# A decay attention with a gated feed-forward behind it: softmax bias taken straight from a masked minimum, remainders moved to VectorE, first half tile spread, last tile in one chain

## The chip, the core and the metric

The kernel runs on one core of a Trainium2 chip. The core has five engines with queues of their own: TensorE (PE in the profile, its weight loads PEld), VectorE (DVE), ScalarE (ACT), GpSimd (POOL) and SyncE (SP), which here only issues DMAs. The metric is the time on the device of one execution, in microseconds (us).

## What is computed

Eight batches with eight heads each, 576 positions, 64 values per head. Attention has a decay (a running sum of log f) added to the scaled scores, a causal mask, a softmax and a product with v. The result, laid out as 4608 rows of 512 values, goes through a two-layer network with hidden width 2048.

```python
scores = scale * np.matmul(q, k.transpose(0, 1, 3, 2))
decay = cum[:, :, :, None] - cum[:, :, None, :]
scores = np.where(causal, -1000000000.0, scores + decay)
scores = scores - np.max(scores, axis=-1, keepdims=True)
attn = np.exp(scores)
attn = attn / (np.sum(attn, axis=-1, keepdims=True) + 1e-09)
x = matmul(attn, v)            # then as rows of 512
h = x @ w_in
g = h * np.clip(h + 3.0, 0.0, 6.0) / 6.0
out = g @ w_out
```

Matrix products of 16-bit operands are made to hold more digits by splitting an operand into a high and a low half (`hi` is the value rounded to 16 bits, `lo` the remainder), so that each product is three matmuls.

## The kernel before

**Work items.** Attention goes through a list `VH`: four items of kind A (batch 0, two heads each, the first 256 positions), eight of kind B (batch 0, the other positions of one head), and 56 of kind F (one head each of batches 1 to 7). Kind F is the function `rows`. For one head it works in two halves (chunks 1, 4 and 0 of the rows, then chunks 2 and 3). A half goes like this: TensorE writes scores to `pn` (L611, L614); VectorE adds the mask, writes `pp` and takes each row's maximum into `mc`, a tile `MF` (L622, a multiply-reduce followed by a read of the accumulator); VectorE makes the exponent's bias `nb` = -max/8 + log(16) in a pass of its own (L628); ScalarE takes exp with that bias (L634) and rounds the result to 16 bits into a buffer `ring` (L651); the remainders are subtractions into the same buffer (L654 for the columns left of the last two blocks, L660 and L665 for what is in front of them, called "the pair" and "the corner" below); SyncE issues a transposing DMA to `pT` (L672). For batch 1 the remainder of chunk 3 stands on GpSimd (`PL_POOL`), for batches 2 to 7 the pairs and the corner do (`B0_POOL`). A head later `av` multiplies `pT` with v into `pav` (L697 to L702; L708 for kinds A and B), divides by the row sums (L726, L729, L732, for batch 0 also L731), splits into halves `xhl` (L737, L738), and `x_move` issues transposing DMAs to `xT` and `xS`.

**Network.** A tile `t` of 512 rows (one batch less 64 rows, which are put together in `xS`) is sixteen units `h_unit` and four units `out_unit`. An `h_unit` is 12 matmuls to `ph` (L786 to L788), then ScalarE `r` (L794), VectorE `r` (L797, the last to read `ph`), ScalarE `gT` high (L798) and VectorE `gT` low (L799). An `out_unit` is 48 matmuls to `po` (L839 to L841), a scaled copy to `o` on ScalarE (L845) and DMAs to the result (L848). Tile 0 is done in two halves of 256 rows: the first after kind A, the second after kind B. `h_short` and a last `out_unit` do the rows in `xS`; for the last batch these are two units of 256 columns with their operand in `vst`.

**Order.** The network's units are generators in a queue; `fill` gives them credit, eight times in each work item, at a rate that is `F_RATE[0]` in kind B, `F_RATE[1]` in batch 1 and follows from what is left after that. Credit sets the place in the written program. A scheduler that goes by its own estimates then orders each engine's instructions, with the place in the written program as the priority; engines run their queues in that order. `behind` tells it to put a matmul after one named before it (used for the last tile's `h_unit`s). In PSUM two buffers hold `pn` and `ps` (tag S), two hold `ph` and `po` (tag mm) and a third is lent to them.

Of the kernel before, what the change touches and what calls it, by code (L numbers as in the profile page):

```python
# [11 lines left out]
F32 = mybir.dt.float32  # L12
# [3 lines left out]
ALU = mybir.AluOpType  # L16
# [4 lines left out]
def kernel(  # L21
# [60 lines left out]
    NQK, NL, NST = 3, 2, 3  # L82
    W_RATE = (8, 2, 4)
    H_COST = 1.05
    F_RATE = (0.6, 0.45)
    PIN = 0
    PIN0 = 1
    LOW_W = 0
# [9 lines left out]
    VH += [("F", n) for n in range(H, NHEAD)]  # L98
    NV = len(VH)
    NRING = 3  # L100
    PL_POOL = ((3, ), ())
    NAT = ((1, 4, 0), (2, 3))
    B0_POOL = ((0, 0), (1, 1))
    W_AHEAD = (4, 5)
    W_ORDER = 0
    POOL_REST = ((0, 0, 0, 0), (0, 0, 0, 0))
# [484 lines left out]
    ringh = [t.bitcast(F16) for t in ring]  # L591
    clean = set()

    def rows(v):
        i, j = v % NQK, v % NL
        n = VH[v][1]
        late = min(n // H, 2) - 1
        pT = p2.tile([P, 3200], F16, tag="PHL", name=f"pT_{v}")
        mc = MF[v % 2]
        nb = p2.tile([P, NCH], F32, tag="nb", name=f"nb_{v}")  # L600
        e0 = 0
        for half in range(2):
            pn = ps_s.tile([P, 1024], F32, tag="S", name=f"pn_{v}_{half}")
# [15 lines left out]
            for x, c in enumerate(NAT[half]):  # L619
                o, r, kw = PLACE[c], RR[c], RB[c] + RR[c]  # L620
                at[c] = w
                nc.vector.tensor_tensor_reduce(  # L622
                    pp[:r, w:w + kw], pn[:r, o:o + kw], W[:r, 4 * P + r - kw:4 * P + r],
                    1.0, -3.0e38, ALU.add, ALU.max, accum_out=mc[:r, e0 + x:e0 + x + 1],
                )
                w += kw
            e1 = e0 + len(NAT[half])
            nc.vector.tensor_scalar(  # L628
                nb[:, e0:e1], mc[:, e0:e1], -0.125, math.log(PSC), op0=ALU.mult, op1=ALU.add
            )  # L630
            for x, c in enumerate(NAT[half]):
                r, kw = RR[c], RB[c] + RR[c]
                x_ = pp[:r, at[c]:at[c] + kw]
                nc.scalar.activation(  # L634
                    x_, x_, AF.Exp, bias=nb[:r, e0 + x:e0 + x + 1], scale=0.125
                )
            e0 = e1
            yield
# [1 line left out]
            def pair(t, a, b):  # L640
                return t[:, a:a + 2 * (b - a)].rearrange("p (n w) -> p n w", n=2)[:, :, 0:64]
# [6 lines left out]
                    clean.add(slot)  # L648
            for c in NAT[half]:
                r, kw, a = RR[c], RB[c] + RR[c], GH[half][c]  # L650
                nc.scalar.copy(hl[:r, h0[c]:h0[c] + kw], pp[:r, at[c]:at[c] + kw])  # L651
                if c:
                    eng = nc.gpsimd if c in PL_POOL[late] else nc.vector
                    eng.tensor_tensor(  # L654
                        hl[:r, a:a + c * P], pp[:r, at[c] + 64:at[c] + kw],
                        hl[:r, h0[c] + 64:h0[c] + kw], op=ALU.subtract,
                    )
            eng = nc.gpsimd if B0_POOL[late][half] else nc.vector
            a, b = NAT[half][:2]
            eng.tensor_tensor(  # L660
                pair(hl, h0[a] - 64, h0[b] - 64), pair(pp, at[a], at[b]), pair(hl, h0[a], h0[b]),
                op=ALU.subtract,
            )
            if 0 in NAT[half]:
                eng.tensor_tensor(  # L665
                    hl[:64, h0[0] - 64:h0[0]], pp[:64, at[0]:at[0] + 64], hl[:64, h0[0]:h0[0] + 64],
                    op=ALU.subtract,
                )

            w = sum((2 * c + 1) * P for c in NAT[half])  # L670
# [14 lines left out]
    def av(v, ph):  # L685
# [146 lines left out]

    def out_unit(s, three, col, rows_, gs=None, cols=(0, DM)):
        g = gT if gs is None else gs
        c = slice(*cols)
        po = mm_tile(f"po_{rows_[0]}_{cols[0]}", three)[:, c]
        ts_ = slice(s * P, (s + 1) * P)
        for fc in range(NFC):
            nc.tensor.matmul(po, g[:, 0, fc, ts_], w2[:, fc, 0, c], start=(fc == 0), stop=False)  # L839
            nc.tensor.matmul(po, g[:, 0, fc, ts_], w2[:, fc, 1, c], start=False, stop=False)  # L840
            nc.tensor.matmul(po, g[:, 1, fc, ts_], w2[:, fc, 0, c], start=False, stop=(fc == NFC - 1))  # L841
# [3 lines left out]
        nc.scalar.activation(o[:, c], po, AF.Copy, scale=scol(col))  # L845
        w = P // len(rows_)
# [248 lines left out]
```

## Time and profile before

| | us |
|---|---|
| median of 3 runs | 1079.81 (1077.97 to 1083.37) |
| the profiled execution, its own time | 1077.53 |
| its span, first to last instruction | 1075.5 |
| PE, DVE, ACT, POOL busy | 1011.0, 746.1, 588.6, 498.6 |

A row of the profile names line, engine, operation, tiles and shape, then count, busy time and mean duration of one in nanoseconds (ns), then the idle time of the engine just before, with what ended it. In the view of stages a row has the stretch in us from the span's start, each engine's busy time in it with its count, the granted TensorE clock as a share (PEclk), the DMA engines' share and GB/s. In the list of waits a row gives who waited for whom: us in total, times, longest. A matmul counts as busy from issue to its modelled end, so that back-to-back matmuls overlap.

### The profile page before, as it was taken

How to read it: one execution, taken by the hardware profiler on the slowest of the kernel's cores; microseconds unless marked ns; L12 is line 12 of the kernel's file. 1: busy time of each engine (PE TensorE's matmuls, PEld its weight loads, DVE VectorE, ACT ScalarE, POOL GpSimd, SP SyncE). 2: the span in 40 equal slices, each digit the busy share in tenths (PEclk: the TensorE clock that was granted, in tenths of full speed). 3: DMA queues.
4: the chain of work that ended last, by engine and by line, in shares of the span. 5: the costliest groups of instructions: out<-in, count | busy, mean ns of one | idle time of the engine just before them, and what ended most of it. 6: DMA issues, size and time to landing. Idle time of an engine off the chain costs nothing.

```text
span 1075.5 us, 20984 instructions
## 1 busy us (share of the span) xinstructions
PE 1011.0 (94%) x7698; PEld 605.3 (56%) x7698; DVE 746.1 (69%) x1903; ACT 588.6 (55%) x1190; POOL 498.6 (46%) x588
## 2 busy tenths in 40 slices
PE   2799898798899999999999999999999999999997
PEld 1568756665455754555555755555555755545545
DVE  7979977998885658966975569867865678405400
ACT  4877745766664547655564556645654566315400
POOL 8655456677544555554454455555535553100000
PEclk9899998999999999999999999999999999999999
DMA  7765233767545564466444465455444354400001
GB/s 245 254 206 161 69 80 81 173 126 150 140 83 114 110 146 85 82 127 151 84 81 103 102 140 111 94 120 137 79 105 95 74 95 79 89 30 1 1 5 45
DMA packets 248418, 114.36 MB, mean 106 GB/s; under 512 B 224788, under 2 KB 226124, under 8 KB 248316
## 3 DMA queue, kind: packets, MB, share of 16 engines
q1 hardware_dynamic: 248316, 113.03, 46.9%
q8 instruction: 60, 0.98, 0.4%
q14 instruction: 42, 0.34, 0.1%
HBM read 47.93 MB, written 9.73 MB: 54 GB/s over the span
## 4 chain that ended last, share of the span: by engine, by line
PE 60%; DVE 21%; issue 6%; DMA 5%; ACT 5%; POOL 2%; SPq 1%; DVEq 0%; ACTq 0%; POOLq 0%
PE po L839 10%; PE po L841 10%; PE po L840 10%; PE ph L786 5%; PE ph L787 5%; PE ph L788 5%; DVE pp L622 4%; DVE gT L799 3%; DVE ring L654 2%; PE pn L611 2%; DMA vst<-in_vS_dram 2%; PE pn L614 2%; DVE r L797 2%; ACT pp L634 2%; DVE nb L628 2%
## 5 line engine op out<-in xcount | busy, mean ns | idle before, releaser
L634 ACT ACTIVATE pp<-pp,nb 128x192 f32<-128x192 f32 x280 | 138.8, 552 | 144.7 <-DVE nb L628 143.7
L786 PE MATMUL ph<-xT,w 128*128 128x512 f16 (+1 forms) x576 | 202.5, 361 | 13.6 <-DVE r L797 9.2
L839 PE MATMUL po<-w,gT 128*128 128x512 f16 x560 | 208.8, 380 | 1.6 <-DVE r L797 0.8
L840 PE MATMUL po<-w,gT 128*128 128x512 f16 x560 | 208.2, 380 | 0.0
L841 PE MATMUL po<-w,gT 128*128 128x512 f16 x560 | 208.1, 380 | 0.0
L787 PE MATMUL ph<-xT,w 128*128 128x512 f16 (+1 forms) x576 | 201.3, 360 | 0.0
L788 PE MATMUL ph<-xT,w 128*128 128x512 f16 (+1 forms) x576 | 201.3, 360 | 0.0
L654 DVE TENSOR_TENSOR ring<-pp,ring 128x128 f16<-128x128 f32 (+2 forms) x216 | 148.2, 700 | 69.7 <-ACT ring L651 69.3
L447 POOL TENSOR_SCALAR TK<-ST 64x576 fp32r<-64x576 f32 (+1 forms) x68 | 54.9, 807 | 283.2 <-issue 206.6
L622 DVE CUSTOM_DVE_ANT_0 pp<-pn,W 128x192 f32<-128x192 f32 x280 | 123.8, 481 | 27.5 <-PE pn L614 27.2
L798 ACT CAST gT<-r 128x512 f16<-128x512 f32 (+1 forms) x144 | 81.6, 568 | 91.9 <-DVE r L797 91.5
L799 DVE TENSOR_TENSOR gT<-r,gT 128x512 f16<-128x512 f32 (+1 forms) x144 | 116.1, 807 | 19.7 <-ACT gT L798 19.1
L611 PE MATMUL pn<-TK,TQ 68*128 68x192 f32 x336 | 123.9, 383 | 5.9 <-DVE MF L622 5.1
L797 DVE SCALAR_TENSOR_TENSOR r<-r,ph 128x512 f32<-128x512 f32 (+1 forms) x144 | 89.2, 619 | 56.0 <-ACT r L794 55.9
L794 ACT ACTIVATE r<-ph,bias_r,SC 128x512 f32<-128x512 f32 (+1 forms) x144 | 103.5, 723 | 18.5 <-PE ph L788 15.3
L614 PE MATMUL pn<-T,T 128*128 128x192 f32 x336 | 113.3, 363 | 0.0
L651 ACT CAST ring<-pp 128x192 f16<-128x192 f32 x280 | 113.3, 450 | 0.0
L460 POOL TENSOR_TENSOR T<-ST,T 64x576 fp32r<-64x576 f32 (+1 forms) x68 | 105.8, 1556 | 5.2
L660 POOL TENSOR_TENSOR ring<-pp,ring 128x128 f16<-128x128 f32 x96 | 55.0, 572 | 90.9 <-ACT ring L651 58.9
L457 POOL TENSOR_TENSOR T<-ST,TQ 64x576 fp32r<-64x576 f32 (+2 forms) x68 | 94.8, 1394 | 4.9
L787 PEld LDWEIGHTS <-w 128*128 128x128 f16 x576 | 56.9, 99 | 62.5 <-issue 20.9
L841 PEld LDWEIGHTS <-gT 128*128 128x128 f16 x560 | 54.7, 98 | 66.0 <-issue 5.5
(156 smaller groups left out, 2084.8 us busy)
## 6 DMA issues: line engine op xcount, KB each, us to landing
ST<-in_qk_dram SPq DMA_DIRECT2D x64, 288.0 KB
out_dram<-o SPq DMA_DIRECT2D x33, 256.0 KB
ring<-in_w_out_dram SPq DMA_DIRECT2D x16, 512.0 KB
vst<-in_vS_dram SPq DMA_DIRECT2D x7, 1040.0 KB
ring<-in_w_in_dram SPq DMA_DIRECT2D x9, 512.0 KB
w<-in_w_in_dram SPq DMA_DIRECT2D x7, 512.0 KB
vst<-in_vS_dram SPq DMA_DIRECT2D x14, 130.0 KB
pT<-ring SPq DMA_TRANSPOSE x112
```

Source lines behind the costliest of these rows:

```text
L611: nc.tensor.matmul(dst, TQ[i][0:D + 4, qs], TK[i][0:D + 4, a:e], start=True, stop=False)
L614: nc.tensor.matmul(dst, T7[j][:, qs], T1[j][:, a:e], start=False, stop=True)
L622: nc.vector.tensor_tensor_reduce(pp[:r, w:w + kw], pn[:r, o:o + kw], W[:r, 4 * P + r - kw:4 * P + r], 1.0, -3.0e38, ALU.add, ALU.max, accu ...
L634: nc.scalar.activation(x_, x_, AF.Exp, bias=nb[:r, e0 + x:e0 + x + 1], scale=0.125)
L654: eng.tensor_tensor(hl[:r, a:a + c * P], pp[:r, at[c] + 64:at[c] + kw], hl[:r, h0[c] + 64:h0[c] + kw], op=ALU.subtract,)
L786: nc.tensor.matmul(ph, w1[0][:, cc, fs_], xh, start=(cc == 0), stop=False)
L787: nc.tensor.matmul(ph, w1[0][:, cc, fs_], xl, start=False, stop=False)
L788: d = nc.tensor.matmul(ph, w1[1][:, cc, fs_], xh, start=False, stop=(cc == NCC - 1))
L799: nc.vector.tensor_tensor(gT[:, 1, fc, c0:c1], r, gT[:, 0, fc, c0:c1], op=ALU.subtract)
L839: nc.tensor.matmul(po, g[:, 0, fc, ts_], w2[:, fc, 0, c], start=(fc == 0), stop=False)
L840: nc.tensor.matmul(po, g[:, 0, fc, ts_], w2[:, fc, 1, c], start=False, stop=False)
L841: nc.tensor.matmul(po, g[:, 1, fc, ts_], w2[:, fc, 0, c], start=False, stop=(fc == NFC - 1))
```

## The change

Four things are changed.

- **The masked maximum.** The masked pass now multiplies by -0.125 and takes the minimum, so that `pp` holds minus an eighth of the masked score and its row minimum is -max/8 itself. ScalarE takes exp with scale -1 and that minimum as the bias; `nb` and its pass are gone. The factor 16 that was in the bias moves to the rounding pass (a copy with scale 16, L651) and to the remainders (`low`: 16 times the exponential minus the high half).
- **Remainders.** `PL_POOL` and `B0_POOL` are gone: every remainder is on VectorE, written as one scalar-tensor-tensor operation.
- **Batch 0's row sums.** The multiplication by the scale of v is folded into the pass that adds the small constant (L726), so that L731 falls away.
- **Pace and end.** `F_RATE[0]` goes from 0.6 to 0.45, which spreads the first half tile's units over kind B. The last tile's `out_unit`s are put one behind the other by `behind`.

```diff
-    F_RATE = (0.6, 0.45)
+    F_RATE = (0.45, 0.45)
-    PL_POOL = ((3, ), ())
-    B0_POOL = ((0, 0), (1, 1))
...
+    def low(out_, x, hi):
+        nc.vector.scalar_tensor_tensor(out_, x, PSC, hi, op0=ALU.mult, op1=ALU.subtract)
...
                 nc.vector.tensor_tensor_reduce(
                     pp[:r, w:w + kw], pn[:r, o:o + kw], W[:r, 4 * P + r - kw:4 * P + r],
-                    1.0, -3.0e38, ALU.add, ALU.max, accum_out=mc[:r, e0 + x:e0 + x + 1],
+                    -0.125, 3.0e38, ALU.add, ALU.min, accum_out=mc[:r, e0 + x:e0 + x + 1],
                 )
-            nc.vector.tensor_scalar(
-                nb[:, e0:e1], mc[:, e0:e1], -0.125, math.log(PSC), op0=ALU.mult, op1=ALU.add
-            )
...
-                    x_, x_, AF.Exp, bias=nb[:r, e0 + x:e0 + x + 1], scale=0.125
+                    x_, x_, AF.Exp, bias=mc[:r, e0 + x:e0 + x + 1], scale=-1.0
...
-                nc.scalar.copy(hl[:r, h0[c]:h0[c] + kw], pp[:r, at[c]:at[c] + kw])
+                nc.scalar.activation(
+                    hl[:r, h0[c]:h0[c] + kw], pp[:r, at[c]:at[c] + kw], AF.Copy, scale=PSC
+                )
                 if c:
-                    eng = nc.gpsimd if c in PL_POOL[late] else nc.vector
-                    eng.tensor_tensor(
+                    low(
                         hl[:r, a:a + c * P], pp[:r, at[c] + 64:at[c] + kw],
-                        hl[:r, h0[c] + 64:h0[c] + kw], op=ALU.subtract,
+                        hl[:r, h0[c] + 64:h0[c] + kw],
                     )
-            eng = nc.gpsimd if B0_POOL[late][half] else nc.vector
             a, b = NAT[half][:2]
-            eng.tensor_tensor(
-                pair(hl, h0[a] - 64, h0[b] - 64), pair(pp, at[a], at[b]), pair(hl, h0[a], h0[b]),
-                op=ALU.subtract,
-            )
+            low(
+                pair(hl, h0[a] - 64, h0[b] - 64), pair(pp, at[a], at[b]),
+                pair(hl, h0[a], h0[b]),
+            )
...
+            sums = pav[:, p0:p1, vo + D:vo + D + 1]
+            if b == 0:
+                nc.vector.tensor_scalar(rs, sums, PSC * 1e-9, scol(IV), op0=ALU.add, op1=ALU.mult)
+            else:
+                nc.vector.tensor_scalar(rs, sums, PSC * 1e-9, None, op0=ALU.add)
             nc.vector.reciprocal(rs, rs)
-            if b == 0:
-                nc.vector.tensor_scalar(rs, rs, scol(SV + b), None, op0=ALU.mult)
...
     def out_unit(s, three, col, rows_, gs=None, cols=(0, DM)):
+        last = col in (UO + B - 1, UX + B - 1)
...
-            nc.tensor.matmul(po, g[:, 0, fc, ts_], w2[:, fc, 0, c], start=(fc == 0), stop=False)
+            with behind(last and fc == 0):
+                nc.tensor.matmul(po, g[:, 0, fc, ts_], w2[:, fc, 0, c], start=(fc == 0), stop=False)
...
+        if last:
+            chain.append(d.ins)
```

Three places show how the instructions move. The line numbers of the changed kernel are one to four lower than before (L693 is L697 before, L610 is L611, L837 is L839, L621 is L622, L593 is every remainder).

TensorE, around the end of the first half tile's `out_unit`s. `po` are their products, `pav` here those of kind B's last head, `pn` the scores of the second head of batch 1. Before:

```order
L840 MATMUL po_0_1525<-w_115,gT 128x512
L841 LDWEIGHTS gT
L841 MATMUL po_0_1525<-w_115,gT 128x512
L708 MATMUL pav<-v_111,pf_1566 128x96 x6
L708 MATMUL pav<-xT_118,pf_1566 128x96
L708 MATMUL pav<-v_111,pf_1566 64x96 x3
L708 MATMUL pav<-xT_118,pf_1566 64x96 x2
L611 MATMUL pn_0_1744<-TK_97,TQ_94 128x192
```

Now:

```order
L838 MATMUL po_0_1624<-w_115,gT 128x512
L704 MATMUL pav<-v_111,pf_1506 128x96
L839 LDWEIGHTS gT
L839 MATMUL po_0_1624<-w_115,gT 128x512
L704 MATMUL pav<-xT_118,pf_1506 128x96
L704 MATMUL pav<-v_111,pf_1506 64x96 x3
L704 MATMUL pav<-xT_118,pf_1506 64x96 x2
L610 MATMUL pn_0_1691<-TK_97,TQ_94 128x192
L613 MATMUL pn_0_1691<-T_100,T_102 128x192
L610 MATMUL pn_0_1691<-TK_97,TQ_94 128x320
```

Before, all 96 matmuls of the two units stand ahead of the last head's `pav`; now these stand between `po` matmuls, and 30 of the 96 come behind them, in turn with the next heads' scores.

VectorE, one head of a late batch: `r` and `gT` belong to `h_unit`, `pp_0` and `pp_1` to the head's two halves. Before:

```order
L797 SCALAR_TENSOR_TENSOR r_0_0_6119<-r_0_0_6119,ph_0_0_6060 128x512
L628 TENSOR_SCALAR nb_6132<-MF_109 128x3
L799 TENSOR_TENSOR gT<-r_0_0_6119,gT 128x512
L622 ISA pp_1_6194,MF_109<-pn_1_6189,W 128x320
L622 ISA MF_109 128x1
L622 ISA pp_1_6194,MF_109<-pn_1_6189,W 128x448
L622 ISA MF_109 128x1
L797 SCALAR_TENSOR_TENSOR r_1_0_6169<-r_1_0_6169,ph_1_0_6156 128x512
L654 TENSOR_TENSOR ring_124<-pp_0_6142,ring_124 128x128
```

Now:

```order
L793 SCALAR_TENSOR_TENSOR r_0_0_6022<-r_0_0_6022,ph_0_0_5963 128x512
L593 SCALAR_TENSOR_TENSOR ring_124<-pp_0_6044,ring_124 128x128
L795 TENSOR_TENSOR gT<-r_0_0_6022,gT 128x512
L593 SCALAR_TENSOR_TENSOR ring_124<-pp_0_6044,ring_124 128x512
L593 SCALAR_TENSOR_TENSOR ring_124<-pp_0_6044,ring_124 128x2x64
L621 ISA pp_1_6095,MF_109<-pn_1_6090,W 128x320
L621 ISA MF_109 128x1
L621 ISA pp_1_6095,MF_109<-pn_1_6090,W 128x448
L621 ISA MF_109 128x1
L793 SCALAR_TENSOR_TENSOR r_1_0_6070<-r_1_0_6070,ph_1_0_6057 128x512
```

The first half's remainders now stand ahead of the second half's masked passes; over the whole program this is so for 48 of 56 heads, and was for 26.

TensorE, the program's end. Before:

```order
L840 MATMUL po_0_12370<-w_115,gT 128x512
L841 LDWEIGHTS gT
L841 MATMUL po_0_12370<-w_115,gT 128x512
L839 LDWEIGHTS gT
L839 MATMUL po_0_12370<-w_115,gT 128x512
L840 LDWEIGHTS gT
```

Now:

```order
L838 LDWEIGHTS vst
L838 MATMUL po_256_12291<-w_115,vst 128x256
L839 LDWEIGHTS vst
L839 MATMUL po_256_12291<-w_115,vst 128x256
L837 LDWEIGHTS vst
L837 MATMUL po_256_12291<-w_115,vst 128x256
```

Before, the last four units are interleaved and a unit of 512 columns ends last; now six units of 48 matmuls follow each other, and a unit of 256 columns is the last.

More of the change, by code (lines that the diff above doesn't have):

```diff
@@ L596, in rows @@
         n = VH[v][1]
-        late = min(n // H, 2) - 1
         pT = p2.tile([P, 3200], F16, tag="PHL", name=f"pT_{v}")
         mc = MF[v % 2]
-        nb = p2.tile([P, NCH], F32, tag="nb", name=f"nb_{v}")
         e0 = 0
@@ L650, in rows @@
                 r, kw, a = RR[c], RB[c] + RR[c], GH[half][c]
-                nc.scalar.copy(hl[:r, h0[c]:h0[c] + kw], pp[:r, at[c]:at[c] + kw])
+                nc.scalar.activation(
+                    hl[:r, h0[c]:h0[c] + kw], pp[:r, at[c]:at[c] + kw], AF.Copy, scale=PSC
+                )
                 if c:
-                    eng = nc.gpsimd if c in PL_POOL[late] else nc.vector
-                    eng.tensor_tensor(
+                    low(
                         hl[:r, a:a + c * P], pp[:r, at[c] + 64:at[c] + kw],
-                        hl[:r, h0[c] + 64:h0[c] + kw], op=ALU.subtract,
+                        hl[:r, h0[c] + 64:h0[c] + kw],
                     )
-            eng = nc.gpsimd if B0_POOL[late][half] else nc.vector
             a, b = NAT[half][:2]
-            eng.tensor_tensor(
-                pair(hl, h0[a] - 64, h0[b] - 64), pair(pp, at[a], at[b]), pair(hl, h0[a], h0[b]),
-                op=ALU.subtract,
+            low(
+                pair(hl, h0[a] - 64, h0[b] - 64), pair(pp, at[a], at[b]),
+                pair(hl, h0[a], h0[b]),
             )
             if 0 in NAT[half]:
-                eng.tensor_tensor(
-                    hl[:64, h0[0] - 64:h0[0]], pp[:64, at[0]:at[0] + 64], hl[:64, h0[0]:h0[0] + 64],
-                    op=ALU.subtract,
+                low(
+                    hl[:64, h0[0] - 64:h0[0]], pp[:64, at[0]:at[0] + 64],
+                    hl[:64, h0[0]:h0[0] + 64],
                 )
@@ L838, in out_unit @@
         for fc in range(NFC):
-            nc.tensor.matmul(po, g[:, 0, fc, ts_], w2[:, fc, 0, c], start=(fc == 0), stop=False)
+            with behind(last and fc == 0):
+                nc.tensor.matmul(po, g[:, 0, fc, ts_], w2[:, fc, 0, c], start=(fc == 0), stop=False)
             nc.tensor.matmul(po, g[:, 0, fc, ts_], w2[:, fc, 1, c], start=False, stop=False)
-            nc.tensor.matmul(po, g[:, 1, fc, ts_], w2[:, fc, 0, c], start=False, stop=(fc == NFC - 1))
+            d = nc.tensor.matmul(
+                po, g[:, 1, fc, ts_], w2[:, fc, 0, c], start=False, stop=(fc == NFC - 1)
+            )
             if fc % 2 and fc < NFC - 1:
                 yield 2.0 - H_COST
+        if last:
+            chain.append(d.ins)
         o = p2.tile([P, DM], F32, tag="o", name=f"o_{rows_[0]}_{cols[0]}")
```

2 lines of the change are left out of this document (removed).

## The prediction

> **What bounds the kernel now.** I read the stages first, then who waits for whom, then the end. The stages have busy times of PE, PEld, DVE, ACT and POOL, then the granted TensorE clock.
>
> ```profile
> 46.00:138.00 92.00, 85.30 (x599) 67.04 (x598) 80.55 (x222) 70.68 (x146) 52.62 (x61) 0.94 0.48 146
> 138.00:172.00 34.00, 32.37 (x223) 19.79 (x221) 22.91 (x74) 15.62 (x35) 17.74 (x17) 1.00 0.26 64
> 172.00:220.00 48.00, 36.72 (x375) 30.78 (x375) 45.99 (x130) 32.81 (x78) 34.39 (x32) 0.86 0.67 148
> 220.00:300.00 80.00, 73.83 (x605) 42.44 (x603) 71.03 (x186) 50.70 (x107) 50.25 (x56) 1.00 0.67 139
> 300.00:930.00 630.00, 624.63 (x4972) 356.94 (x4969) 458.06 (x1148) 356.66 (x721) 309.07 (x373) 1.00 0.52 104
> ```
>
> From 300 us on TensorE is busy 624.63 of 630 us, VectorE only 458.06: that is a TensorE bound, and no saving on another engine can be worth more there than the 5.4 us that are missing. From 172 to 220 us it is the other way round: VectorE 45.99 of 48, TensorE 36.72. Between, 138 to 172, VectorE is idle for a third of the time. The change adds and removes no matmul, so it can only take waits of TensorE away, or add some. The list of TensorE's waits says which there are; first those from 138 to 300 us:
>
> ```profile
> PE pn L611 <- DVE MF L622: 5.1, 2, 3.2
> PE ph L786 <- DMA xT<-xhl: 4.4, 1, 4.4
> PE pav L697 <- DMA pT<-ring: 2.9, 4, 1.1
> PE ph L786 <- DVE r L797: 2.3, 7, 0.4
> ```
>
> and all of those from 300 to 1046 us:
>
> ```profile
> PE ph L786 <- DVE r L797: 5.3, 10, 1.0
> ```
>
> So some 15 us of waits lie in the passage from batch 0 to batch 1, and 5.3 us in the long rest. The two long ones cost more than their length. Here are kind B's last `pav` matmuls, the matmul that ended the 4.36 us wait, and the clock behind both waits:
>
> ```profile
> 162.83 0.63 PE L708 MATMUL pav<-xT,pf 128*64 128x96 f32 x4
> ...
> 175.53 0.37 PE L786 MATMUL ph<-xT,w 128*128 128x256 f16 x1 [4.36 <-DMA xT<-xhl]
> ...
> 175.50:181.90 6.40, 5.60 (x26) 4.20 (x26) 5.53 (x21) 4.07 (x10) 3.77 (x3) 0.50 0.79 148
> 210.00:213.50 3.50, 0.39 (x5) 0.28 (x3) 3.50 (x8) 1.49 (x4) 2.40 (x2) 0.88 0.77 145
> 213.50:219.50 6.00, 5.93 (x52) 4.78 (x53) 6.00 (x20) 4.54 (x10) 4.36 (x5) 0.50 0.65 157
> ```
>
> After each of the two pauses the clock stands at 0.50 for about 6 us while TensorE is busy 5.60 and 5.93 us. At full clock that work takes half, so each pause costs some 2.8 to 3.0 us more.
>
> **The end, row by row.** First the last two matmuls, then the one that waited for a buffer, then ScalarE's last copies:
>
> ```profile
> 1067.93 0.38 PE L840 MATMUL po<-w,gT 128*128 128x512 f16 x1
> 1068.14 0.38 PE L841 MATMUL po<-w,gT 128*128 128x512 f16 x1
> ...
> 1047.52 0.38 PE L839 MATMUL po<-w,gT 128*128 128x512 f16 x1 [0.78 <-ACT o L845]
> ...
> 1068.61 1.05 ACT L845 ACTIVATE o<-po,SC 128x512 f32<-128x512 f32 x2 [18.32 <-PE po L841]
> 1071.43 0.47 ACT L845 ACTIVATE o<-po,SC 128x256 f32<-128x256 f32 x1 [1.77 <-DMA out_dram<-o]
> ```
>
> The last matmul ends at 1068.52, the span at 1075.5: 7.0 us. Three units end together, so their three copies queue up, and the third waits 1.77 us for an `o` buffer until an earlier DMA has left it. With the units in a chain only the unit of 256 columns is left at the end. From the start of its copy to the span's end is 1075.5 - 1071.43 = 4.1 us today, and a copy starts 0.09 us after its matmul: 4.2 us in place of 7.0, **-2.8 us**. The 0.78 us wait at 1047.52 came from three interleaved units holding all buffers; a chain holds two at most, **-0.8 us**. This term is the safest. What could be lost is cover for the first unit's operand, but its last chunk is read only after 45 matmuls at 0.21 us.
>
> **The pace.** The order shows what 0.45 does: the `po` matmuls no longer stand as one block ahead of kind B's last `pav`; 30 of 96 come behind it, with 0.21 us each, 6.3 us of work. The 4.36 us wait at 175.5 was for `xT` made from that `pav`, which ended at 163.5. Its way (division, split, transposing DMA) took 12 us, while TensorE had scores, 27 matmuls of `ph` and a `pav` to do and then nothing. Now it has the 6.3 us of `po` more and has done fewer `ph` before: the 4.4 us are covered. With them goes the half clock behind: **-4.4 - 2.8 = -7.2 us**. The 3.2 us wait of `pn` at 213 is VectorE's (3.50 of 3.50 us busy): the masked pass that frees the scores' buffer comes late in a full queue. VectorE was idle for 11 of the 34 us from 138 to 172, and the new order gives it the next heads' scores there; the queue is shorter later. I take half of wait and clock, -(3.2 + 3.0) / 2 = **-3.1 us**, between none and 6.2. What is late next: the first head of batch 1 has its `pav` ahead of the second half tile now, with less between its scores and its `pav`. The four waits for `pT` were 2.9 us; I let them grow by **+2 us** (bounds 0 and twice 2.9).
>
> **The bias and the remainders.** Prices, and then two pairs of one shape:
>
> ```profile
> L628 DVE TENSOR_SCALAR nb<-MF 128x2 f32<-128x2 f32 x56 | 19.9, 356 | 0.3
> L628 DVE TENSOR_SCALAR nb<-MF 128x3 f32<-128x3 f32 x56 | 18.4, 329 | 0.7
> L660 POOL TENSOR_TENSOR ring<-pp,ring 128x128 f16<-128x128 f32 x96 | 55.0, 572 | 90.9 <-ACT ring L651 58.9 <-PE pn L614 6.6 <-PE pn L611 6.2
> L665 POOL TENSOR_TENSOR ring<-pp,ring 64x64 f16<-64x64 f32 x48 | 22.1, 460 | 0.4
> L660 DVE TENSOR_TENSOR ring<-pp,ring 128x128 f16<-128x128 f32 x16 | 8.9, 558 | 0.0
> L665 DVE TENSOR_TENSOR ring<-pp,ring 64x64 f16<-64x64 f32 x8 | 3.0, 374 | 0.0
> ...
> 153.52 0.28 DVE L660 TENSOR_TENSOR ring<-pp,ring 128x128 f16<-128x128 f32 x1
> 174.03 0.75 DVE L660 TENSOR_TENSOR ring<-pp,ring 128x128 f16<-128x128 f32 x1
> ```
>
> VectorE loses 19.9 + 18.4 = 38.3 us. It takes over 96 pairs and 48 corners: 96 x 0.558 + 48 x 0.374 = 71.5 us at the mean. The eight remainders of chunk 3 in batch 1 and the folded L731 are small and of opposite sign. Net +33 us, all but a little of it beside TensorE's 624.63. The pair's price moves between 0.28 and 0.75 us; the long one stands where GpSimd is busier (34.39 of 48 us from 172, 17.74 of 34 before). Since 55.0 + 22.1 us leave GpSimd, the lower price gets more frequent: bounds 96 x 0.28 - 38.3 = -11 us without the corners, and 96 x 0.75 + 48 x 0.374 - 38.3 = +52 us. The Trainium skill (SBUF — State Buffer, section SBUF: two separate sides) says why: a VectorE operation with two SBUF inputs and a GpSimd operation take one pair of ports in turn, each for a whole instruction. The trace agrees with its 0.28 beside 0.75; by that rule every moved remainder can be stopped in VectorE's queue by one of GpSimd's, which before only GpSimd's own queue paid for.
>
> What ScalarE gains is latency:
>
> ```profile
> ACT pp L634 <- DVE nb L628: 115.7, 54, 6.5
> ```
>
> From 300 to 930 us it stood 115.7 us waiting for `nb`; now an exp goes as soon as its own chunk's minimum is there. TensorE's 5.3 us of waits are for `r`, which queues behind those exps; I take **-1 us** of it, between -5.3 and the slow rival below. ScalarE's rounding pass becomes a copy with a factor:
>
> ```profile
> L634 ACT ACTIVATE pp<-pp,nb 128x576 f32<-128x576 f32 x56 | 42.6, 760 | 0.0
> L651 ACT CAST ring<-pp 128x576 f16<-128x576 f32 x56 | 37.3, 666 | 0.0
> L289 ACT ACTIVATE w<-low 128x512 f16<-128x512 f32 x12 | 6.8, 592 | 1.3 <-PE low L288 1.3
> ```
>
> At worst each of 280 costs 0.094 us more, as exp does: +26 us on ScalarE, at 55% of the span. L289 is a copy with a constant factor and takes 592 for 512 elements, nearer to the plain cast: I take 0.
>
> **Sum.** -2.8 - 0.8 - 7.2 - 3.1 + 2 - 1 = -12.9 us. The profiled execution took 1077.5 us and would take 1064.6; its time lies 2.3 us under the median, so the median comes to **1067 us**.
>
> **Rivals.** (1) *Only the end gains*: VectorE's queue, not TensorE's order, makes `xT` late, so the pause moves and stays as long. For it: 12 us from `pav` to `xT`, and VectorE full from 172 on. Against: VectorE's idle time just before. 1079.8 - 3.6 = 1076 us.
>
> (2) *Slower: VectorE waits for ScalarE inside its own queue.* In 48 heads the first half's remainders now stand ahead of the second half's masked passes, so these, and `r` behind them, wait for the exp and the rounding. Two rows bear on it:
>
> ```profile
> DVE ring L654 <- ACT ring L651: 64.8, 47, 1.7
> ...
> 420.00:460.00 40.00, 38.35 (x294) 21.14 (x293) 35.45 (x85) 24.94 (x50) 22.96 (x27) 1.00 0.49 94
> ```
>
> Such a wait is 1.4 us in the mean already (64.8 / 47). Where a batch begins VectorE is at 35.45 of 40; three heads (630 us over 48 heads, 13 us each) with 1 us more waiting and 0.7 us more work each make 40.5: full, and TensorE waits for `r`. From that point each such head passes on its 1 us: six batches by three heads, +18 us. With the end (-3.6) and half the pace's -8.3: 1079.8 + 18 - 3.6 - 4.1 = 1090 us. Against it: outside those stretches VectorE has 27% spare.
>
> (3) *The thinner filling opens new pauses in kind B.* From 46 to 138 us TensorE is at 85.30 of 92 and has few units to spare. Two pauses like the one at 213 (3.2 + 3.0 us) cost 12 us: 1079 us. The Trainium skill (TensorE: Matmul & The Clock Gate, section HAM oscillation) warns of idle gaps over about 3.4 us, after which the clock halves; here a 3.2 us wait was enough. Against this rival: the `ph` units' places among kind B's heads hardly move in the order.
>
> **How the numbers follow.** The forecast 0.64, rival (1) 0.16, (2) 0.11, (3) 0.09. All waits from 138 to 300 us and the end together would give some 25 us: low 1055. The high end takes in (1) and (3): 1081; (2) and the part under 1055 stay out. A difference under 0.5%, 5.4 us, is about what a measurement here can't tell from none. Faster by more: nearly all of the forecast, a third of (1): 0.70; slower: (2): 0.12; between: 0.18.
>
> **What would show it.** Right: the last copy within 0.1 us of the last matmul and 4.2 us from there to the end; no wait over 1 us for `xT` and no clock of 0.50 near 175 us; GpSimd near 412 us busy (498.6 less 55.0, 22.1 and a little); VectorE near 780 (746.1 and 33). Wrong: 300 to 930 us with more than 10 us of TensorE waiting for `r` or for `MF` (rival 2); a granted clock under 0.90 from 46 to 138 us (rival 3); the rounding pass at 760 in place of 666.

## The result, and the profile after

The changed kernel takes **1066.69 us** in the median of 4 runs (1065.58 to 1067.12), the kernel before 1079.34 beside it: a ratio of 0.988 (95% interval 0.985 to 0.990), 12.7 us less. Its profiled execution took 1066.79 us, with a span of 1065.0. One execution of the kernel with the chain alone (2641.57 us) and one of the kernel with pace and minimum (2637.01 us, its profiled one) took more than twice as long as every other and are left out of the times below.

Three places in TensorE's own order cut both spans into five stretches: the first matmul of the first half tile's ninth `h_unit`, of the ninth `h_unit` of tile 1, and of the first `h_unit` of the last tile; then the last matmul. "Passage" below is from the first of them to the second (kind B's second half, batch 1), "long stretch" from the second to the third.

| us | to the first place | passage | long stretch | last tile | after the last matmul | span |
|---|---|---|---|---|---|---|
| before | 109.2 | 175.9 | 671.1 | 112.3 | 7.0 | 1075.5 |
| after | 114.1 | 169.2 | 666.0 | 111.4 | 4.3 | 1065.0 |
| difference | +4.9 | -6.7 | -5.1 | -0.9 | -2.7 | -10.5 |

The first two columns are not steady. The changed kernel and the same without its chain have one order of TensorE, VectorE and ScalarE up to the last tile, and yet 114.1 and 110.5 us in the first column and 169.2 and 171.1 in the second; the kernel before and the one with the chain alone have 109.2 and 111.8, then 175.9 and 175.8. So the +4.9 is not shown to be the change's, and the -6.7 is good to about 2 us. The stages after, in the same stretches as before (busy time of PE, PEld, DVE, ACT, POOL; granted clock, DMA share, GB/s):

```profile
46.00:138.00 92.00, 84.65 (x565) 66.12 (x563) 74.39 (x203) 62.65 (x133) 47.53 (x57) 0.91 0.49 150
138.00:172.00 34.00, 33.93 (x236) 22.36 (x236) 33.30 (x82) 25.68 (x50) 20.60 (x18) 1.00 0.26 62
172.00:220.00 48.00, 36.36 (x400) 31.26 (x399) 47.64 (x129) 33.73 (x79) 32.96 (x30) 0.93 0.77 164
220.00:300.00 80.00, 75.72 (x624) 43.20 (x622) 74.48 (x196) 53.16 (x110) 37.70 (x36) 1.00 0.67 136
300.00:930.00 630.00, 627.57 (x5020) 359.17 (x5020) 482.60 (x1184) 365.05 (x718) 249.69 (x244) 1.00 0.51 104
```

From 138 to 172 us VectorE now works 33.30 of 34 us (22.91 before). The next heads' scores are not what came there. VectorE's list for this stretch, first before, then now, has ten masked passes (L622, now L621) in both; the new work is splitting the network's weights (L295, now L293) and remainders:

```profile
L295 DVE SCALAR_TENSOR_TENSOR w<-w,SC 128x512 f16<-128x512 f32 x6 | 6.3, 1058 | 0.0
L622 DVE CUSTOM_DVE_ANT_0 pp<-pn,W 128x192 f32<-128x192 f32 (+4 forms) x10 | 4.4, 476 | 0.0
```

```profile
L293 DVE SCALAR_TENSOR_TENSOR w<-w,SC 128x512 f16<-128x512 f32 x16 | 13.7, 892 | 0.2 <-ACT w L282 0.2
L593 DVE SCALAR_TENSOR_TENSOR ring<-pp,ring 128x128 f16<-128x128 f32 (+4 forms) x12 | 7.6, 688 | 0.4 <-ACT ring L647 0.4
L621 DVE CUSTOM_DVE_ANT_0 pp<-pn,W 128x192 f32<-128x192 f32 (+4 forms) x10 | 4.4, 479 | 0.0
```

Behind it VectorE is as full as it was: 47.64 of 48 (45.99 before). What TensorE waits for from 138 to 300 us, in the changed kernel:

```profile
PE ph L782 <- DVE r L793: 5.3, 3, 3.0
PE pn L610 <- DVE MF L621: 4.7, 3, 2.2
PE ph L782 <- DMA xT<-xhl: 1.9, 1, 1.9
...
PE pav L693 <- DMA pT<-ring: 1.0, 2, 0.7
```

The wait for `xT` fell from 4.4 to 1.9 us, those for `pT` from 2.9 to 1.0. That for `MF` stayed (5.1, now 4.7), and `r` went from 2.3 to 5.3. One half-clock stretch of two is left behind 138 us, at 199.9 (windows view of the changed kernel):

```profile
172.00:182.00 10.00, 7.48 (x90) 6.35 (x88) 9.64 (x33) 7.95 (x18) 6.97 (x6) 1.00 0.76 163
196.50:199.90 3.40, 0.98 (x4) 0.69 (x5) 3.40 (x10) 2.23 (x5) 0.66 (x2) 1.00 0.96 249
199.90:206.70 6.80, 4.46 (x48) 3.67 (x48) 6.80 (x14) 1.78 (x5) 6.14 (x6) 0.50 0.36 65
```

A sum can be made of this. From 138 to 300 us TensorE was busy 32.37 + 36.72 + 73.83 = 142.9 us before, of which 5.60 + 5.93 us at half clock are worth half: 137.2 us of work. Now it is 33.93 + 36.36 + 75.72 = 146.0 us, less half of 4.46: 143.8. That is 6.6 us more work done in the same time, beside the 6.7 us by which the passage is shorter.

The long stretch, first before, then after, by the same two places in the program:

```profile
285.10:956.20 671.10, 664.75 (x5222) 376.74 (x5221) 473.29 (x1183) 369.31 (x745) 315.01 (x380) 1.00 0.50 102
```

```profile
283.30:949.30 666.00, 663.57 (x5226) 376.88 (x5225) 498.58 (x1220) 377.80 (x742) 255.86 (x250) 1.00 0.50 101
```

TensorE was idle for 671.10 - 664.75 = 6.4 us of it before and for 2.4 us now, with 25 us more of VectorE's work beside it. From 300 us to the last matmul the list has one entry (before 5.3 us in 10 waits); under it what ScalarE's exp and VectorE's remainders wait for from 300 to 930 us:

```profile
PE ph L782 <- DVE r L793: 2.4, 6, 0.7
...
ACT pp L630 <- DVE MF L621: 70.3, 56, 4.2
...
DVE ring L593 <- ACT ring L647: 48.4, 51, 1.6
```

The exp waited 115.7 us for `nb`, and waits 70.3 us for the minimum itself; the remainders waited 64.8 us for the rounding in VectorE's queue, and wait 48.4. The end, in the timelines of TensorE (its last matmul) and of ScalarE (its last two copies):

```profile
1060.44 0.27 PE L839 MATMUL po<-w,vst 128*128 128x256 f16 x1
```

```profile
1055.56 0.47 ACT L847 ACTIVATE o<-po,SC 128x256 f32<-128x256 f32 x1 [4.55 <-PE po L839]
1060.80 0.47 ACT L847 ACTIVATE o<-po,SC 128x256 f32<-128x256 f32 x1 [4.77 <-PE po L839]
```

The last copy starts 0.09 us behind the last matmul's end at 1060.71, and the span ends 4.3 us behind that end. Prices and totals: the exp, the rounding pass, a remainder of 128 by 128 (the pairs and one of 128 columns share that shape), and the page's line of engines:

```profile
L630 ACT ACTIVATE pp<-pp,MF 128x576 f32<-128x576 f32 x56 | 42.7, 762 | 0.9 <-DVE MF L621 0.9
L647 ACT ACTIVATE ring<-pp 128x576 f16<-128x576 f32 x56 | 37.5, 670 | 0.0
...
L593 DVE SCALAR_TENSOR_TENSOR ring<-pp,ring 128x128 f16<-128x128 f32 x168 | 90.3, 537 | 2.4 <-ACT ring L647 0.8
```

```profile
PE 1008.7 (95%) x7698; PEld 606.0 (57%) x7698; DVE 777.0 (73%) x1927; ACT 600.3 (56%) x1190; POOL 424.7 (40%) x436
```

### The profile page after: what moved, and what is told of

It reads as the page before. It is cut to its first block, busy times and chain, and to the rows that moved or that the text cites. A ratio compares the mean times of both kernels' runs of the same rounds, so it can differ in the third digit from the quotient of the medians.

```text
span 1065.0 us, 20477 instructions
## 1 busy us (share of the span) xinstructions
PE 1008.7 (95%) x7698; PEld 606.0 (57%) x7698; DVE 777.0 (73%) x1927; ACT 600.3 (56%) x1190; POOL 424.7 (40%) x436
## 4 chain that ended last, share of the span: by engine, by line
PE 64%; DVE 21%; DMA 5%; ACT 4%; issue 4%; POOL 1%; SPq 1%; DVEq 0%; ACTq 0%; POOLq 0%
PE po L837 10%; PE po L839 10%; PE po L838 10%; PE ph L782 6%; PE ph L783 5%; PE ph L784 5%; DVE ring L593 5%; DMA vst<-in_vS_dram 3%; DVE pp L621 3%; PE pn L613 3%; PE pn L610 3%; DVE gT L795 2%; DVE r L793 2%; DVE vm L364 2%; PE phs L808 1%
## 5 line engine op out<-in xcount | busy, mean ns | idle before, releaser
L593 DVE SCALAR_TENSOR_TENSOR ring<-pp,ring 128x128 f16<-128x128 f32 x392 | 236.6, 643 | 54.0 <-ACT ring L647 52.2
L837 PE MATMUL po<-w,gT 128*128 128x512 f16 x560 | 209.0, 381 | 0.4 <-DVE r L793 0.4
L839 PE MATMUL po<-w,gT 128*128 128x512 f16 x560 | 208.3, 380 | 0.0
L630 ACT ACTIVATE pp<-pp,MF 128x192 f32<-128x192 f32 x280 | 147.8, 554 | 87.5 <-DVE MF L621 86.7
L621 DVE CUSTOM_DVE_ANT_0 pp<-pn,W 128x192 f32<-128x192 f32 x280 | 123.5, 481 | 18.2 <-PE pn L613 17.9
L610 PE MATMUL pn<-TK,TQ 68*128 68x192 f32 x336 | 124.7, 385 | 6.2 <-DVE MF L621 4.7
L647 ACT ACTIVATE ring<-pp 128x192 f16<-128x192 f32 x280 | 120.0, 459 | 1.5
L795 DVE TENSOR_TENSOR gT<-r,gT 128x512 f16<-128x512 f32 (+1 forms) x144 | 100.4, 699 | 26.1 <-ACT gT L794 24.7
L458 POOL TENSOR_TENSOR T<-ST,T 64x576 fp32r<-64x576 f32 (+1 forms) x68 | 105.4, 1549 | 5.1
L455 POOL TENSOR_TENSOR T<-ST,TQ 64x576 fp32r<-64x576 f32 (+2 forms) x68 | 100.1, 1472 | 5.4
L847 ACT ACTIVATE o<-po,SC 128x512 f32<-128x512 f32 (+1 forms) x37 | 24.8, 670 | 125.0 <-PE po L839 123.7
L839 PEld LDWEIGHTS <-gT 128*128 128x128 f16 x560 | 54.6, 98 | 65.6 <-issue 6.9
```

The costliest lines, as they stand in the source:

```text
L593: nc.vector.scalar_tensor_tensor(out_, x, PSC, hi, op0=ALU.mult, op1=ALU.subtract)
L610: nc.tensor.matmul(dst, TQ[i][0:D + 4, qs], TK[i][0:D + 4, a:e], start=True, stop=False)
L621: nc.vector.tensor_tensor_reduce(pp[:r, w:w + kw], pn[:r, o:o + kw], W[:r, 4 * P + r - kw:4 * P + r], -0.125, 3.0e38, ALU.add, ALU.min, ac ...
L630: nc.scalar.activation(x_, x_, AF.Exp, bias=mc[:r, e0 + x:e0 + x + 1], scale=-1.0)
L795: nc.vector.tensor_tensor(gT[:, 1, fc, c0:c1], r, gT[:, 0, fc, c0:c1], op=ALU.subtract)
L839: d = nc.tensor.matmul(po, g[:, 1, fc, ts_], w2[:, fc, 0, c], start=False, stop=(fc == NFC - 1))
```

## The experiments

### One part of the change at a time

Theory: the chain is worth what the end shows, the pace what the passage shows, the bias and the remainders next to nothing.

**The pace alone**, in the kernel before:

```diff
-    F_RATE = (0.6, 0.45)
+    F_RATE = (0.45, 0.45)
```

> The kernel before with one edit, F_RATE[0] 0.45 in place of 0.6. The prediction's theory: most of the gain is this one's, the wait for xT at 175 us and the half clock behind it go, 1079 - 8 = 1071 us. The rival that the trace of the changed kernel suggests (at 283 us it is no further than the kernel before: 24th half of scores 1.5 us later, second half of tile 1 1.8 us earlier): the pause is filled but others open in VectorE's full queue, 1077 to 1081 us.

Measured: **1088.32 us**, ratio 1.008 (1.005 to 1.010). The theory falls: without the rest of the change the pace makes the kernel slower by 9 us. The loss is not in the long stretch (671.2 us, as before) but ahead of it: the first place is reached at 114.8 us and the passage takes 181.3. The stages of this kernel:

```profile
46.00:138.00 92.00, 80.50 (x531) 62.19 (x530) 80.48 (x215) 67.53 (x139) 51.28 (x61) 0.90 0.49 148
...
220.00:300.00 80.00, 68.61 (x558) 41.01 (x557) 70.14 (x188) 45.70 (x99) 49.62 (x56) 0.91 0.68 142
```

TensorE is short by 4.8 us from 46 to 138 us, at a clock of 0.90, and by 5.2 us from 220 to 300. The largest pause is one row of TensorE's timeline (start, duration, then in brackets the idle time ahead; "issue" means that the profile names nothing that ended it):

```profile
242.12 0.50 PE L611 MATMUL pn<-TK,TQ 68*128 68x192 f32 x1 [6.65 <-issue]
```

VectorE's timeline over the same time, up to the masked pass that ends 0.11 us before and, as far as can be told, frees the scores' buffer:

```profile
235.99 1.88 DVE L654 TENSOR_TENSOR ring<-pp,ring 128x512 f16<-128x512 f32 x1
237.79 0.99 DVE L660 TENSOR_TENSOR ring<-pp,ring 128x128 f16<-128x128 f32 x1
238.71 1.75 DVE L398 SCALAR_TENSOR_TENSOR v<-vst,SC,v 128x320 f16<-128x320 f32 x1
...
241.80 0.21 DVE L622 CUSTOM_DVE_ANT_0 pp<-pn,W 64x64 f32<-64x64 f32 x1
```

Three operations with two inputs take 4.6 us between them; the pair's 0.99 us stands beside 0.28 for the same operation at 241.95, when the queue has passed. So the masked pass of 0.21 us stands behind the stretched ones, and from 237.8 us on, inside the pause, the clock is at half for 10.2 us.

**The chain alone**, the part of the diff in `out_unit` and nothing else:

```diff
+        last = col in (UO + B - 1, UX + B - 1)
...
+            with behind(last and fc == 0):
...
+        if last:
+            chain.append(d.ins)
```

> The kernel before with one edit, the last tile's output units put behind each other. Both theories: 3.6 us less, 1075.5 us; from the last matmul to the end of the span 4.2 us in place of 7.0, no wait for a buffer among the last units. If the scheduler makes something else of it (an operand not ready at the start of the chain): no change.

Measured: **1075.52 us**, 0.997 (0.995 to 0.999), 3.6 us less. From the last matmul to the end 4.2 us, the last tile 111.4: the two numbers of the whole change.

**The masked minimum alone.** The bias comes straight from the minimum; the factor is 1 in place of 16, so that the remainders can stay as they were, on GpSimd too (a matter of rounding):

```diff
-PSC = 2.0 ** 4
+PSC = 1.0
...
-                    1.0, -3.0e38, ALU.add, ALU.max, accum_out=mc[:r, e0 + x:e0 + x + 1],
+                    -0.125, 3.0e38, ALU.add, ALU.min, accum_out=mc[:r, e0 + x:e0 + x + 1],
...
-            nc.vector.tensor_scalar(nb[:, e0:e1], mc[:, e0:e1], -0.125, math.log(PSC), ...)
...
-                    x_, x_, AF.Exp, bias=nb[:r, e0 + x:e0 + x + 1], scale=0.125
+                    x_, x_, AF.Exp, bias=mc[:r, e0 + x:e0 + x + 1], scale=-1.0
```

> The kernel before with the masked minimum as the bias and without nb, remainders where they were (GpSimd for the pairs). To need no factor in the rounding pass, the factor 16 is 1 here in all of the kernel, which changes a little rounding and no instruction's size. The prediction's theory: 1 us of TensorE's waits for r, 1078 us. The rival: the 7 us that the changed kernel gains between 283 and 930 us are from here, 1072 to 1074 us, and TensorE's waits for r after 300 us fall from 5.3 to about 2.4 us.

Measured: **1078.54 us**, 0.999 (0.996 to 1.001): no difference that can be told. In the trace the long stretch is shorter by 4.4 us all the same, with TensorE idle for 2.4 us of it:

```profile
287.80:954.50 666.70, 664.27 (x5240) 377.56 (x5237) 454.63 (x1094) 377.89 (x744) 325.45 (x383) 1.00 0.51 102
```

Ahead of it, the profiled execution is 2.7 us later (111.3 and 176.5 us), no more than the first two columns vary by themselves, and the median of the runs lies 2.9 us above that execution. What takes the gain back there isn't settled.

**The remainders alone**, all moved to VectorE, with `nb` kept:

```diff
-    PL_POOL = ((3, ), ())
+    PL_POOL = ((), ())
...
-    B0_POOL = ((0, 0), (1, 1))
+    B0_POOL = ((0, 0), (0, 0))
```

> The kernel before with one edit, all remainders on VectorE as plain subtractions, nb kept. The prediction's theory: VectorE busy +60 to +70 us, hidden behind TensorE after 300 us, 1079 us +-2. The slow rival of the prediction (VectorE's queue waits for ScalarE where a batch begins): over 1085 us, with over 10 us of TensorE's waits for r or MF after 300 us.

Measured: **1082.78 us**, 1.002 (1.000 to 1.004), which can hardly be told from none. The long stretch takes 670.7 us, as before, although VectorE works 505.5 us of it in place of 473.3: its 32 us more are hidden there. Its profiled execution is 6.3 us longer than that of the kernel before, most of it ahead of the first place (112.7 us), where the column is unsteady, and in the passage (178.7 us, +2.8).

By themselves the four give +9.2, -3.6, -0.6 and +3.7 us: 8.7 us slower together. The change is 12.7 us faster. So either they are not independent, or the fifth part, the folded row sums of batch 0, does the rest. The next kernels take one part out of the whole.

### The whole without one part

**Without the pace** (0.6 again):

```diff
-    F_RATE = (0.45, 0.45)
+    F_RATE = (0.6, 0.45)
```

> The changed kernel with F_RATE[0] back at 0.6. The prediction's theory: 8 us are lost, 1075 us, with a pause for xT of over 4 us near 175 us. The rival (pace is worth nothing in sum): 1066 to 1068 us.

Measured: **1074.97 us**, 0.996 (0.994 to 0.998). The passage takes 177.6 us in place of 169.2; the long stretch, 667.9, keeps most of its gain. In the whole change the pace is worth 8.3 us. The pause for `xT` of over 4 us that was expected near 175 us did not come. From 138 to 300 us TensorE's list has it with 1.3 us, behind others; the stages show a lower clock than the changed kernel's 1.00, 0.93 and 1.00:

```profile
PE ph L782 <- DVE r L793: 4.5, 2, 3.4
PE pn L610 <- DVE MF L621: 3.4, 2, 1.7
...
PE ph L782 <- DMA xT<-xhl: 1.3, 1, 1.3
...
138.00:172.00 34.00, 30.98 (x170) 18.83 (x169) 23.18 (x62) 16.45 (x35) 14.15 (x13) 0.95 0.29 64
172.00:220.00 48.00, 40.65 (x445) 34.57 (x444) 44.48 (x128) 34.22 (x78) 37.46 (x35) 0.89 0.71 145
220.00:300.00 80.00, 73.80 (x595) 43.66 (x595) 73.24 (x192) 50.48 (x107) 40.36 (x37) 0.96 0.67 134
```

**Without the chain** (`last = False`):

> The changed kernel without the chain of the last tile's output units. Both theories: 3.6 us are lost, 1070.3 us; 7.0 us from the last matmul to the end of the span.

Measured: **1070.76 us**, 0.992 (0.989 to 0.995); 7.5 us from the last matmul to the end. The chain is worth 4.1 us here and 3.6 alone: it adds up with the rest in both.

**Without the masked minimum.** The maximum, `nb` and the factor in the bias are back; the remainders stay on VectorE as plain subtractions:

```diff
-                    -0.125, 3.0e38, ALU.add, ALU.min, accum_out=mc[:r, e0 + x:e0 + x + 1],
+                    1.0, -3.0e38, ALU.add, ALU.max, accum_out=mc[:r, e0 + x:e0 + x + 1],
...
+            nc.vector.tensor_scalar(nb[:, e0:e1], mc[:, e0:e1], -0.125, math.log(PSC), ...)
...
-        nc.vector.scalar_tensor_tensor(out_, x, PSC, hi, op0=ALU.mult, op1=ALU.subtract)
+        nc.vector.tensor_tensor(out_, x, hi, op=ALU.subtract)
...
```

> The changed kernel with nb's pass back (masked maximum, exp with bias nb and the factor 16 in it, plain rounding, plain subtractions on VectorE). The prediction's theory: 1 us is lost, 1068 us. The rival (the gain after 283 us is nb's): 1073 us or more, TensorE's waits for r after 300 us at 5 us or more.

Measured: **1081.95 us**, 1.003 (1.001 to 1.005): 15 us above the whole change. The passage takes 175.3 us and the long stretch 676.8, the longest of all. The long stretch and its first 112 us, in this kernel:

```profile
287.90:964.70 676.80, 666.64 (x5226) 377.68 (x5225) 507.49 (x1318) 368.40 (x743) 253.77 (x250) 1.00 0.49 101
288.00:400.00 112.00, 106.47 (x894) 62.91 (x893) 86.42 (x221) 57.95 (x119) 43.09 (x42) 0.98 0.50 100
```

TensorE is idle for 10.2 us of the long stretch, 5.5 of them in its first 112 us. VectorE's remainders wait for the rounding as long as in the kernel before, from 300 to 930 us (list of waits of this kernel):

```profile
DVE ring L593 <- ACT ring L651: 64.9, 50, 2.1
```

**Without the moved remainders**: on GpSimd again where they had been, with the factor 1 as above; pace, minimum, chain and the folded row sums stay:

```diff
-PSC = 2.0 ** 4
+PSC = 1.0
...
+    PL_POOL = ((3, ), ())
...
+    B0_POOL = ((0, 0), (1, 1))
```

> The changed kernel with the remainders where they were (pairs on GpSimd for batches 2 to 7, chunk 3 for batch 1) and the factor 16 as 1 in all of the kernel, so that the rounding pass and the subtractions are plain. The prediction's theory: the move is hidden, so no change, 1066 to 1068 us, VectorE busy 70 us less. The rival (the move itself shortens the way from exp to pT, and GpSimd's lock on the ports falls away): 1069 us or more.

Measured: **1066.38 us**, 0.988 (0.985 to 0.992): the same time as the whole change, with VectorE at 451.9 us of the long stretch and not 498.6. In the whole change, moving the remainders is worth nothing.

### The pace, with and without the rest

What is left open is why 0.45 costs 9 us in one kernel and brings 8.3 in the other. Pace and minimum may need each other, the folded row sums may matter, or 0.45 in the kernel before is one bad order.

**Pace and minimum, nothing else** (the first and third diffs together):

> The kernel before with two parts of the change, the first half tile's pace of 0.45 and the masked minimum as the exponent's bias (factor 1 in place of 16, a matter of rounding), and without the chain, the folded row sums and the moved remainders. Alone the pace gave 1088.3 us and the minimum 1078.5. Theory: these two need each other; with both the passage is as short as in the whole change (about 169 us from the first half tile's middle to the middle of the second tile) and only the chain's 3.6 us are missing: 1070 us. Rival one: they add up, 1088.3 - 0.6 = 1088 us, and what made the whole change fast was the folded pass of batch 0's row sums, or the chain's other order. Rival two: half of it, 1079 us, which leaves the cause open.

Measured: **1077.49 us**, 0.997 (0.995 to 0.999). Neither: 10.8 us under the pace alone, yet 7.5 us above what it would be if only the chain were missing (1066.4 + 3.6 = 1070). What stands between is the folded pass of batch 0's row sums, beside the remainders' move, which was worth nothing above. The written orders show what it does: with the pace alone, and with pace and minimum, TensorE's instructions around the end of batch 0 are the same, with 36 `po` matmuls in one block ahead of the last two heads' `pav` of kind B; with the fold added the scheduler lays them out as in the changed kernel, in pieces of at most 20 between scores and `pav`. The fold removes a small VectorE pass for each item of batch 0; the 7.5 us are more likely that other order than the passes saved, though the fold wasn't timed by itself, and no kernel separates the two. With the minimum and without the fold, the pace is worth little: 1078.5 us at 0.6 and 1077.5 at 0.45.

**Other paces**, in the changed kernel and in the one before:

```diff
-    F_RATE = (0.45, 0.45)
+    F_RATE = (0.525, 0.45)
```

> The changed kernel with a pace of 0.525, halfway between 0.6 (1075.0 us) and 0.45 (1066.7 us). Theory of a trend (more of the first half tile's work behind kind B, the later its results wait for): 1071 us, between the two. Rival (the pace acts through where each instruction happens to fall in the order, not through how much is moved): a time outside 1067 to 1075, with other waits of TensorE from 138 to 300 us than either neighbour has.

> The changed kernel with a pace of 0.375, thinner than the change. Theory of a trend: the gain goes on at the same slope or levels off, 1062 to 1067 us. Rival of the accidental place: outside that, most likely slower, 1070 to 1080 us, with half-clock stretches of TensorE between 138 and 300 us that the changed kernel does not have. A third reading, too thin a filling in kind B: slower as well, but with the loss between 46 and 138 us, where the granted clock would be under 0.90.

> The kernel before with a pace of 0.525. There 0.6 gave 1079.3 and 0.45 gave 1088.3 us. Theory of a trend with the bias pass in place (thinner is slower, since VectorE is full behind kind B): 1084 us. Rival of the accidental place: outside 1079 to 1088, above all a time under 1076, which would show that the slow 0.45 was one bad order and not the pace itself.

Measured: 1069.4 us (0.990, 0.987 to 0.993), 1066.68 (0.989, 0.986 to 0.992) and 1074.0 (0.996, 0.994 to 0.998). In one table, with the passage from the profiles:

| `F_RATE[0]` | 0.6 | 0.525 | 0.45 | 0.375 |
|---|---|---|---|---|
| kernel before, us | 1079.3 | 1074.0 | **1088.3** | |
| its passage | 175.9 | 172.8 | **181.3** | |
| changed kernel, us | 1075.0 | 1069.4 | 1066.7 | 1066.7 |
| its passage | 177.6 | 172.7 | 169.2 | 170.8 |

From 0.6 to 0.525 both kernels gain, 5.3 and 5.6 us, and the changed kernel levels off from 0.45 on. The theory of a trend against the kernel before (1084 us) falls: a thinner pace helps there too. The 0.45 in the kernel before is the one that stands out, by some 17 us (it lies 21.6 us above the changed kernel, where 0.6 and 0.525 lie 4.3 and 4.6 above). So the pace by itself is not what costs. Nor is TensorE's order by itself: with pace and minimum it is the same until 175 us of this kernel's profile, up to the half tile's last `po`, and the time is 10.8 us lower. The slow time comes where this pace meets the pass for `nb`; which waits make up the 17 us was not taken apart. No pace tried beats the changed kernel by more than can be told.

## Why the prediction was right, and where not

The forecast was 1067 us and the time is 1066.7. Its sum was -12.9 us: -3.6 at the end, -8.3 in the passage, -1 in the long stretch. Three terms, one by one:

**The end** (-2.8 and -0.8): right within a tenth. After the last matmul 7.0 became 4.3 us, the last tile 112.3 became 111.4. The chain alone and the change without it show the same.

**The pace** (-7.2 - 3.1 + 2 = -8.3): near in size, but not for the reasons given. The passage is 6.7 us shorter in the profiled execution, and 4.8 in that of the same order without the chain. Taking the pace out of the change costs 8.3 us, but that is another sum, as it holds with the fold in place.

The wait for `xT` was 4.4 us, is 1.9, and the clock behind it stayed at 1.00: 2.5 + 2.8 = 5.3 us of the 7.2. It is not the pace alone that does this. At 0.6 the wait is 1.3 us with the rest of the change around it, and the list of the kernel with the minimum alone has none at all; the pace alone leaves 0.3 us of it and still loses 9 us.

The step that failed is the 3.1 us: the next heads' scores were to move into VectorE's idle time from 138 to 172 us, so that "the queue is shorter later". Instead ten more weight splits (7.4 us) and more remainders filled that time, the masked passes there stayed ten, and from 172 to 220 VectorE is fuller than before. The wait for the masked pass stayed, its half clock only moved, from 213 to 199.9 us, and the waits for `r` grew by 3.0.

Against that the +2 us for `pT` did not come (those waits fell by 1.9), and from 220 to 300 us TensorE is busy for 75.72 in place of 73.83 us. Errors of both signs nearly cancel.

**The folded row sums** were put at next to nothing. By the kernel with pace and minimum alone, some 7.5 us of the gain do not come without the fold. That is a difference between kernels, not a run of the fold alone, and how it works stays open, but no term of the sum stands for it.

**The bias and the remainders** (-1 in the long stretch): the mechanism was right, the term mis-sized. It measured -5.1. The prediction gave the waits for `r` a bound of -5.3 and took a fifth of it. The runs part the kernels, if by 1 us at the nearest: the seven whose bias comes straight from the minimum take 664.9 to 667.9 us for the long stretch, the five that are otherwise like the kernel before and keep `nb` 668.9 to 671.2, and the changed kernel with `nb` put back 676.8. The prices were right: the rounding pass takes 670 ns where 666 was taken (and 760 was the bound), a remainder 537 where 558 was, VectorE comes to 777.0 us where 780 was expected. The Trainium skill (ScalarE: Activation LUTs, section What ACT_TABLE_LOAD costs) says that a bias read per partition adds some 93 ns to an activation over a constant one; the 762 ns of the exp beside the 670 of the copy with its constant factor agree, though these two passes differ in their function as well.

**What the sum didn't have**: the first 109 us, which became 114 us in the profiled execution. Up to 3.6 us there are within what two executions of one order differ by; the rest wasn't taken apart. In the profiled executions the change brought 10.7 us, in the medians 12.7, and the forecast was made for an execution 2.3 us under the median. So the hit within a third of a microsecond owes something to luck: the long stretch gave 4 us more than forecast and the start took 5 away.

**The rivals.** (1) *Only the end gains*, 1076 us: the kernel with the chain alone is that, 1075.5; the changed kernel isn't, since the other parts gain some 9 us. (2) *VectorE waits for ScalarE inside its own queue*: not in the changed kernel, whose remainders wait less than before (48.4 and 64.8 us), as the exp goes earlier by the pass that is gone. With `nb` kept and the remainders moved in the kernel before, TensorE waits 6.4 us for `r` in the long stretch, under the 10 that were named. With `nb` put back into it, those waits are as long as before (64.9 us) and the time is 1082; that this is the rival's chain of waits was not followed wait by wait, and its place is the first 112 us of the long stretch more than each batch's start. (3) *Thinner filling opens pauses in kind B*: the clock from 46 to 138 us went from 0.94 to 0.91, above the 0.90 that was named, and TensorE's work there from 85.30 to 84.65. With the same pace in the kernel before the work fell to 80.50 us and the clock to 0.90. But it does not go by the thinness: the changed kernel has 82.95 us and 0.89 at the thicker 0.6, and 86.15 us and 0.96 at 0.375. What decides it is open.

**What it named as signs**: the wait for `xT` is 1.9 us where none over 1 us was to be left. GpSimd came to 424.7 us and not 412; the operations that stayed take longer, its two-input add L455 1549 ns where 1464 was the mean (L457 then).

What stays open: how the fold, the pace and the minimum together shorten the passage; why the masked minimum alone shows 4.4 us in the long stretch and 0.6 in the time, and how much of the 15 us in the change without it belongs to the minimum and how much to another order in the passage (+6.1 us there).

## What to carry to other kernels

Cost an edit by the stage that it changes, and then measure it stage by stage between places in the program: the times of four single edits added up to 9 us slower here, while the chain gave 3.6 to 4.1 us at the end whatever stood around it. The earlier bias did not: 4.4 us of the long stretch alone, 10.8 in the whole change. A small edit counts too, as an order can hang on it: the folded pass looked like nothing and, by difference, stands for some 7.5 us. Where a scheduler orders the work by its own estimates, one value of a pacing number is one draw: try its neighbours in both kernels before calling it good or bad, as 0.45 was 9 us worse in one and 8 us better in the other while 0.525 gave 5 us in both. A pass between two engines that is cheap for the busy one (38 us, all hidden) can still be worth removing for the latency that it puts into the other engine's queue.

## What the runs showed of the hardware

The half clock does not need one long pause. In the changed kernel the longest wait ahead of 199.9 us is 2.2 us, but in the 3.4 us ahead of it TensorE was busy for only 0.98 us, and 6.8 us at half clock follow. In the same kernel 3.4 us with 1.87 us of work, whose last 1.5 us are the start of a pause of 1.8, kept the full clock in the next 3.4. In the changed kernel with a pace of 0.375, 1.84 us of work did not keep it, and in the change without the masked minimum 1.47 us did (windows views of these three kernels in turn):

```profile
237.40:240.80 3.40, 1.87 (x12) 0.91 (x10) 3.40 (x8) 0.95 (x4) 1.33 (x1) 1.00 0.36 69
240.80:244.20 3.40, 3.12 (x17) 1.60 (x18) 3.40 (x14) 2.33 (x5) 1.76 (x1) 1.00 0.20 39
...
206.10:209.50 3.40, 1.84 (x15) 1.50 (x14) 3.40 (x10) 2.37 (x6) 0.51 (x1) 0.99 1.05 303
209.50:212.90 3.40, 3.40 (x19) 2.40 (x17) 3.40 (x6) 0.69 (x3) 3.19 (x5) 0.50 1.01 144
...
202.00:205.40 3.40, 1.47 (x12) 1.17 (x12) 3.40 (x5) 2.63 (x7) 0.30 (x1) 1.00 0.46 88
205.40:208.80 3.40, 2.65 (x37) 2.31 (x37) 3.40 (x12) 1.42 (x3) 0.59 (x1) 1.00 0.52 123
```

All the half-clock stretches of the two kernels ahead of 300 us last 3.4 or 6.8 us, and one in the kernel with the pace alone 10.2: a step of 3.4. The Trainium skill (TensorE: Matmul & The Clock Gate, section What's actually happening) describes a window of 3.4 us that runs freely and by which the clock is set. The step agrees; that a window has to be idle doesn't, since 0.98 us of work in it did not keep the clock. So in this passage TensorE's work per 3.4 us tells more than the length of one wait, though with 1.47 us kept and 1.84 halved it gives no sharp limit. A wait of 2.2 us with a gap behind it was followed by as long a stretch of half clock as one of 4.4.
